# Linear attention and a mixture of experts on one core: another written order for the steps ahead of block 20

## The chip, the core and the metric

The kernel runs on one core of one Trainium2 chip. A core has a matrix engine (PE in the profile, its weight loads PEld), a vector engine (DVE), a scalar engine (ACT), a general engine (POOL) and a queue that issues transfers (SP). Each engine takes its own instructions strictly in the order in which the program was written for it, and they wait for each other by semaphores. The metric is the device time of one execution in microseconds. Three runs of the kernel before gave 652.13, 653.10 and 654.62 us, so its median is 653.1 us.

## The reference, cut to what matters

```python
def phi(x):                                   # 128 random features of a head of 64
    proj = np.einsum('bhsd,md->bhsm', x, omega)
    h = proj - np.sum(x * x, axis=-1, keepdims=True) / 2.0
    return np.exp(h - np.max(h, axis=-1, keepdims=True)) / np.sqrt(m)
q_p, k_p = phi(q_s), phi(k_s)                 # 8 batches, 8 heads, 576 positions
kv = np.einsum('bhsm,bhsd->bhmd', k_p, v)
num = np.einsum('bhsm,bhmd->bhsd', q_p, kv)
den = np.einsum('bhsm,bhm->bhs', q_p, np.sum(k_p, axis=2))[..., None] + 1e-06
x = (num / den) as 4608 tokens of 512
...
e_idx = np.argmax(x @ w_gate, axis=1)         # one of 8 experts for each token
h = np.maximum(x[mask] @ w1[e], 0.0)          # 512 -> 1024
out[mask] = gate_w[mask, None] * eom[mask, e, None] * (h @ w2[e])   # 1024 -> 512
```

## The kernel before

The attention is cut into 32 units. A unit is one head of two batches, so 1152 positions in nine tiles of 128; eight units make a group j of 1152 tokens, and there are four groups. The tokens of all groups are sorted by expert into blocks of up to 128 tokens of one expert; 38 blocks are run in this input. Blocks 0 to 24 are listed after groups 0, 1 and 2 (8, 8 and 9 blocks), so that they can run beside the attention of later groups; the rest is listed after the last group.

Nothing is scheduled by a compiler. The program adds 3310 **steps** to a plan (`plan.add`), each with a key, an engine and a function that emits a few instructions. Two strings of the source then set everything: ORDER names the steps by the number under which they were added, in the order in which they are emitted, and BANKS gives a bank of the accumulator memory (PSUM, eight banks) to each tile that needs one, in that same order. `Plan.order` only asserts that the order keeps every dependency and that no bank is in use twice; `emit` calls the steps in it. So a step's place in ORDER, among the steps of its own engine, is its place in that engine's queue. The 38 blocks run under runtime flags, loaded into registers by steps of their own ("flag").

The steps of a unit u, with k (n = 2u) and q (n = 2u+1) beside each other, g = 0, 1, 2 for three tiles each:

- "ld" (SP): loads of the transposed inputs (L519, tile xt), of the plain ones (xn, from unit 8 on) and of v (L523, rawv). Each has two buffers.
- "hi", "lo", "sqa", "sqr" (ACT L487, POOL L494, ACT L500, DVE L505): halves of the inputs in 16 bits, and squares. For units 0 to 7, "lo" is instead a square in 32 bits (L535 on ACT for unit 0, L537 on POOL for the others).
- "pp" (PE L560): the projections, three tiles of k and of q at a time; it takes two banks. Then "mx", "nb" (DVE L582, L588 to L595) and "ex" (ACT L601): maximum, bias, exponentials; "ex" frees the bank.
- "eh", "el", "eT" (ACT L622, POOL L624, SP L678): halves of the exponentials, and the transposition by the DMA engines. Units 0 to 7 are transposed on PE instead ("tq" L651, "th" L656, "tl" L658).
- "kv", "kvh", "kvs", "kt", "ke", "kg", "gh", "gl" (PE L697, ACT L713 or DVE L715, DVE L717, PE L735, ACT L746, PE L740, ACT L753, DVE L758): keys times values, and their product with the gates.
- "pn" (PE L771; .0 is five tiles, .5 four), "xf" (DVE L780, L782, L784), "xh", "xl", "lga" (DVE L801, POOL L805, POOL L821 or L823), "rows" (SP L844): numerator and denominator, division, halves, gate sums, and the store to memory.

After a group: "route", "counts" (PE L948 to L960), "ranks", "places", "gates", "weigh", "table", "assign", "lists", "pid" (PE L1207), "gi", "controls", "advance", nearly all of them small DVE instructions; and flags.

The steps of a block n: "gx" (POOL L1514) gathers its rows, "xt" (SP L1526) transposes them, "hA" and "hB" (PE L1551, 48 matmuls each) are the two halves of the first layer, "relu" and "rest" (ACT L1558, DVE L1562) split the result, "out" (PE L1582, 12 matmuls a half) is the second layer, "os" (ACT L1637) scales and "put" (POOL L1624) stores. Where a block has another expert than the one before, "bring" (SP L1472) loads 2 MB of weights for each layer and "sw" splits them (ACT L422, DVE L426); n.1 is the first layer, n.2 the second. "w0" and "w0h", "w0l" do this for the first expert.

A step is written below as name.u.g or name.n, as in ex.19.1. The steps that the text speaks of, by their number in ORDER: const.state 6 (four DVE copies of a constant, L388 to L391), w0h.1.0 8, ex.0.1 44, nb.0.1 43, tq.0.0 57, pp.1.1 90, kv.0.0 66, pp.9.2 523, kt.8 498, kvh.8 496, ex.18.0 527, counts.0 1926, hi.11.0 631, ex.19.0 539, ex.19.1 543, pp.10.1 579, kt.9 555, the first flag of ACT and DVE 2046, nb.20.2 591, ex.20.2 592, sqa.12 690, advance.0 2043, pp.11.1 636, kv.15.0 909, hA.4 2284, pp.26.1 1547, pn.24.5 1471, kg.16 976, kv.17.0 1031, xl.28 1720, lga.29 1782, vl.31 1881, gx.21 2554, el.63 1883, eT.31 1884, bring.21.1 2550, hA.21 2556, ld.t.19 1112, eT.16 969, hi.19.0 1115.

Of the kernel before, what the change touches and what calls it, by code (L numbers as in the profile page):

```python
# [128 lines left out]
31 0 3 19 86 1 7 87 4 33 5 34 35 36 88 37 48 49 39 40 50 41 8 38 42 51 52 6 45 46 43 9 53 44 2 10 32 16 13 139 47 11  # L129
57 89 90 66 60 54 55 58 56 63 67 92 95 101 96 102 93 97 94 91 141 68 61 103 64 192 140 22 104 12 59 69 62 105 70 71  # L130
106 72 110 14 73 107 108 65 98 74 99 113 142 100 109 111 114 75 119 79 15 145 146 115 76 77 78 154 155 80 81 82 194
116 120 143 147 20 117 156 121 23 17 112 122 148 157 118 83 149 144 123 124 245 28 125 163 126 164 150 195 151 160 127
158 165 161 152 162 153 132 128 18 198 199 207 133 134 129 169 172 159 84 85 247 130 135 131 166 173 167 174 175 136
208 196 200 170 210 171 211 201 202 176 197 168 246 193 25 298 177 209 21 216 178 179 217 203 248 180 204 205 218 260
213 214 251 206 26 215 212 185 181 225 182 252 183 184 226 300 219 249 222 220 227 29 223 186 221 261 187 228 188 263
229 250 230 262 253 224 254 255 189 138 190 137 351 299 269 231 232 256 270 257 264 233 258 24 266 267 301 238 234 259
304 305 271 239 240 235 241 313 265 268 278 279 280 306 275 302 236 237 314 281 276 353 191 272 282 303 283 273 277
242 352 404 1905 316 317 307 27 308 274 284 318 315 285 286 310 354 309 311 312 287 291 322 331 30 292 319 320 293 288
294 289 323 321 332 325 406 243 333 326 324 290 357 366 367 327 334 355 328 329 368 360 361 330 295 369 356 335 296
244 336 337 358 370 363 364 407 1906 405 457 458 359 338 365 362 339 410 344 340 384 411 372 373 345 346 341 342 412  # L140
374 371 343 419 347 348 349 297 385 386 460 408 375 378 381 350 461 376 387 379 382 420 422 377 380 413 383 423 388
409 462 389 421 459 1907 514 515 390 464 391 463 414 392 416 467 425 393 397 571 572 415 417 428 418 426 398 468 479
394 395 469 427 429 424 437 396 399 430 438 517 439 431 434 432 400 401 480 440 518 403 435 433 519 465 441 483 471
436 442 629 516 470 443 466 520 444 445 487 475 446 521 574 576 575 481 476 484 477 447 472 485 448 473 488 449 577
450 478 474 482 494 451 489 452 453 456 454 1921 522 495 486 490 455 402 528 1922 524 536 1923 491 496 497 1924 525
1925 526 529 685 686 628 1908 573 498 523 1934 530 1935 1936 532 533 540 492 499 527 531 1937 500 1926 1927 541 1928
537 1929 534 2008 501 535 633 2009 502 2010 1938 493 538 2011 542 1930 1939 544 2012 1931 1932 2013 545 1940 2014 546
543 547 631 632 551 552 578 553 539 1941 1942 747 630 2015 1933 634 2016 581 2017 554 582 2018 548 583 579 555 580 556
584 549 557 585 2019 586 2020 2021 2022 589 558 688 503 2023 504 2024 587 2025 559 2026 505 550 2030 2027 506 2028 588
2029 2031 2033 2032 2034 2035 597 2036 590 2037 2044 2045 2216 746 2046 2038 635 507 508 2039 509 2040 591 2041 592  # L150
690 2042 2218 2234 689 2219 807 2214 510 2043 593 601 594 598 638 636 599 602 642 595 600 596 603 608 604 639 691 2215
643 751 511 640 650 605 560 564 609 561 644 565 562 566 563 567 637 610 808 687 2230 641 568 611 645 646 612 692 647
648 613 658 659 651 652 660 654 655 707 656 649 614 2250 513 512 569 606 1909 665 666 615 2217 661 749 653 657 662 667
616 695 696 708 697 668 698 693 2220 663 669 2223 699 700 709 701 710 2221 702 721 607 748 2224 670 2222 752 722 750
570 694 617 621 671 2226 715 703 622 2231 618 672 812 810 619 716 2225 811 704 705 711 706 673 717 712 713 623 620
2235 664 2251 930 868 2246 809 929 2232 869 714 782 719 2227 753 813 624 625 2228 626 720 2229 2266 756 2233 757 768
758 718 759 723 754 674 678 760 679 769 761 770 675 772 762 676 680 2236 755 681 677 682 683 627 771 763 726 2237 871
727 2239 1910 764 765 773 774 728 776 777 766 778 2238 729 724 783 872 775 779 767 725 730 814 815 829 2240 843 780
2241 833 821 817 818 834 822 731 873 2242 874 2247 830 781 732 2243 733 823 819 824 820 734 835 844 739 787 788 735
870 990 2248 2267 2262 991 931 736 740 789 790 831 784 934 737 785 684 786 1052 2252 738 741 742 935 836 832 2244 745  # L160
2282 791 816 792 793 875 2255 2249 2253 825 826 827 794 904 932 828 995 795 837 838 839 2254 743 905 2245 933 744 876
882 840 2263 878 879 841 2256 2258 883 880 884 894 895 890 2257 891 842 2264 992 1113 2278 881 896 996 796 800 885 845
801 797 802 2259 803 798 892 799 846 1056 804 848 806 805 849 893 897 850 851 877 936 993 965 886 852 2268 887 1057
888 951 898 939 2260 853 994 2298 966 854 2265 899 900 889 902 901 855 2269 940 941 952 953 856 2270 2271 937 903 942
955 2272 954 2279 2273 938 2274 1174 2283 1911 2280 2294 847 2284 1117 2285 2299 1051 909 910 947 959 911 948 912 949
943 944 945 2275 2286 913 2287 950 946 914 2276 2314 2261 2277 2281 915 857 861 2290 2288 916 906 956 2289 858 907
2291 957 859 917 960 961 958 2295 862 863 860 864 1118 1026 1112 908 2310 1235 2296 1054 997 998 2300 1055 1000 1004
1005 1006 1001 1002 1016 962 963 2292 1017 1018 1012 1013 1007 1178 999 2301 1003 2303 1008 1020 964 2330 2293 2297
967 1019 1009 865 1010 1021 2302 1179 1022 918 1053 2315 867 968 1011 2304 969 2312 1296 2331 2306 922 970 919 920 921
1014 1015 2305 2311 923 924 925 971 1239 1023 926 928 1943 1944 972 1087 1024 1357 1058 2307 1059 1945 1946 1061 1947  # L170
1956 973 1957 1958 2313 2308 1065 927 1025 1027 866 1948 974 1949 1073 1950 1077 1951 975 1959 1114 1173 2328 1952
2047 1062 1960 1063 1066 1953 2316 1954 2048 1078 1961 1962 1079 2049 1074 1955 1075 2050 1067 1963 1028 1064 1115
1029 1088 1116 1031 1032 976 2317 977 1964 1030 1175 2326 1912 1033 2051 978 2319 1034 2052 2053 2054 2318 1240 2055
2056 1080 1068 1076 2320 1148 2057 979 1060 1035 983 2322 2058 2321 2059 1300 1176 2327 1036 1149 1177 2060 1069 2063
2061 1070 2062 980 984 2064 1081 2065 985 2066 1037 2069 1071 2070 2067 981 2068 2072 982 2073 1038 2323 1418 1234
1295 2071 2074 1039 2075 986 2076 2077 987 2078 2079 2083 2080 1082 2081 1040 1119 1072 2329 2324 1085 1044 1083 1122
1041 1045 1123 1042 1134 1046 1084 2332 988 2309 2346 2362 1124 1047 1043 1048 1301 1089 1125 1120 1086 1121 2335 1126
2333 2082 1127 1128 2334 1138 1139 1130 1135 1140 1131 1136 1142 2085 1361 1129 1049 1090 1092 2347 2084 1479 2342
1091 1093 2338 1237 2336 1137 1141 1143 1144 1094 2337 1238 989 1050 1132 1095 1145 1133 1096 1180 1097 1181 1098 1209
1146 1183 1099 2339 1187 1195 1188 1184 1196 1185 1186 1147 2325 1210 1100 1199 2343 1189 1362 1182 1191 1203 1190  # L180
2340 2348 1105 1236 1356 2344 1913 1422 1150 2378 1151 1197 1200 1192 1193 1198 2345 1106 1204 1201 1205 2349 1206
1202 1298 2360 2363 1540 1152 2358 1299 2350 1423 1483 2351 1153 1154 1101 1417 2379 1601 1102 1107 1108 1103 1104
2354 2352 1270 1194 2353 1155 1156 1271 1241 1157 1207 1158 1208 1256 1244 1242 1159 2355 1248 1160 1249 1250 1245
1246 1257 1260 2359 1161 1109 1247 1251 1211 1110 1212 1358 2374 1162 1166 1167 1261 1262 1258 1163 2361 1263 1259
2356 1214 1168 1215 2364 1169 2365 1216 1164 1165 1170 1217 2376 1213 1297 2394 2341 2357 1243 1218 2367 1302 1219
# [1553 lines left out]
```

## Time and profile before

| | us |
|---|---|
| median of three runs | 653.1 |
| the profiled execution | 655.51 |
| its span, first to last instruction | 653.5 |
| PE busy in the span | 608.4 |
| DVE, ACT, POOL busy | 414.9, 414.5, 339.8 |
| mean granted clock of PE | 0.98 |

The profile is of one execution, 2.4 us above the median. Its page has the busy time of each engine, the granted clock of PE in 40 slices, the chain that ended last, and groups of instructions by line. Behind it stands the trace, which is asked for waits ("engine line waited for: us in total, times, longest us"), for stretches of time (busy time and, in brackets, the number of instructions of each engine; PEclk is the granted share of PE's clock, DMA the mean busy share of the 16 DMA engines) and for single instructions in order of time ("start us, us, engine line op out<-in xcount", with idle time of the engine before it and its releaser in square brackets). A matmul's end is modelled, so short idle times of PE are a little too short.

### The profile page before, as it was taken

What the parts mean: (1) busy time and instruction counts of PE and PEld (TensorE: products, weight loads), DVE (VectorE), ACT (ScalarE), POOL (GpSimd) and SP (SyncE); (2) the same over time, 40 slices, a digit from 0 to 9 for tenths busy, and PEclk for the clock granted to TensorE, in tenths of its full rate; (3) what the DMA queues carried; (4) which work ended last, traced back from release to release, by engine and by line L of the source; (5) the groups of instructions that cost most, each with busy time, mean ns of one, the idle gap of its engine ahead of it and who ended that gap; (6) DMA issues with size and microseconds to landing.
All of it is one profiled execution on the core that took longest, in us unless ns stands there. A gap on an engine that the chain in (4) does not pass through costs nothing. (4 is left out here: it accounts for less than half of the span.)

```text
span 653.5 us, 22348 instructions
## 1 busy us (share of the span) xinstructions
PE 608.4 (93%) x8748; PEld 475.2 (73%) x8748; DVE 414.9 (63%) x1253; ACT 414.5 (63%) x970; POOL 339.8 (52%) x235
## 2 busy tenths in 40 slices
PE   5999977799999999999999899999999899999994
PEld 5898866677776776777767677777777676767673
DVE  4879798767678888666799767662774341070125
ACT  4977697689887967968986687854441341161134
POOL 1233444569883788789867587876321221222111
PEclk9999998599999999999999999999999999999999
DMA  8453669898998988979997958557936855833380
GB/s 290 146 177 116 190 235 250 206 207 265 266 369 201 164 237 243 249 221 256 271 245 192 228 147 182 150 113 171 335 97 180 229 93 101 308 65 90 89 311 16
DMA packets 145893, 129.08 MB, mean 198 GB/s; under 512 B 104270, under 2 KB 127440, under 8 KB 144464
## 3 DMA queue, kind: packets, MB, share of 16 engines
q1 hardware_dynamic: 139760, 107.45, 64.1%
q0 software_dynamic: 5984, 19.72, 8.8%
q8 instruction: 85, 1.39, 0.9%
q14 instruction: 64, 0.52, 0.3%
HBM read 83.86 MB, written 19.30 MB: 158 GB/s over the span
## 5 line engine op out<-in xcount | busy, mean ns | idle before, releaser
L1551 PE MATMUL ph<-xt,w1h 128*128 128x128 f16 (+1 forms) x2432 | 205.5, 217 | 6.2 <-issue 3.7
L1551 PE MATMUL ph<-xt,w1l 128*128 128x128 f16 (+1 forms) x1216 | 200.6, 217 | 3.0 <-issue 1.7
L601 ACT ACTIVATE ef<-pp,nb 128x128 f32<-128x128 f32 x576 | 164.7, 383 | 46.1 <-DVE nb L595 30.1
L1551 PEld LDWEIGHTS <-w1h 128*128 128x128 f16 x2432 | 180.7, 98 | 15.1 <-issue 8.4
L582 DVE TENSOR_REDUCE pp<-pp 128x3 f32<-128x384 f32 x192 | 104.1, 558 | 34.6 <-PE pp L560 24.5
L1562 DVE SCALAR_TENSOR_TENSOR hl<-ph,hh 128x512 f16<-128x512 f32 (+1 forms) x76 | 50.6, 665 | 111.2 <-ACTq L1480 76.3
L1551 PEld LDWEIGHTS <-w1l 128*128 128x128 f16 x1216 | 118.0, 98 | 3.6 <-DVE w1l L426 1.8
L624 POOL TENSOR_TENSOR es<-ef,es 128x1152 f16<-128x1152 f32 x44 | 104.6, 2381 | 18.7 <-ACT es L622 9.9
L1514 POOL DMA_INDIRECT gx<-rows,gi x38 | 40.6, 1068 | 140.8 <-ACT os L1637 110.7
L1582 PE MATMUL po<-w2h,hl 128*128 128x512 f16 x280 | 106.1, 379 | 1.4 <-DVE hl L1562 1.4
L1582 PE MATMUL po<-w2h,hh 128*128 128x512 f16 x280 | 106.3, 380 | 0.7 <-DVE nb L595 0.7
L1582 PE MATMUL po<-w2l,hh 128*128 128x512 f16 x280 | 106.1, 379 | 0.0
L1582 PEld LDWEIGHTS <-hh 128*128 128x128 f16 x560 | 52.0, 99 | 55.3 <-DVE hl L1562 0.9
L1558 ACT ACTIVATE hh<-ph 128x512 f16<-128x512 f32 (+1 forms) x76 | 44.4, 585 | 72.6 <-PE ph L1551 63.7
L494 POOL TENSOR_TENSOR xlo<-xt,xhi 128x1152 f16<-128x1152 f32 x24 | 57.1, 2378 | 21.6 <-ACT xhi L487 19.0
L805 POOL TENSOR_TENSOR xs<-xf,xs 128x576 f16<-128x576 f32 x32 | 41.9, 1312 | 40.2 <-DVE xs L801 17.3
L1637 ACT ACTIVATE os<-po,gx 128x512 f32<-128x512 f32 (+1 forms) x36 | 24.8, 690 | 59.6 <-PE po L1582 59.4
L1582 PEld LDWEIGHTS <-hl 128*128 128x128 f16 x280 | 27.4, 98 | 35.7 <-DVE hl L1562 3.2
L622 ACT CAST es<-ef 128x1152 f16<-128x1152 f32 x44 | 50.9, 1160 | 2.2 <-ACTq L1475 0.7
L560 PE MATMUL pp<-omh,xhi 64*128 64x128 f16 x432 | 42.7, 225 | 7.4 <-DVE xf L784 4.4
L771 PE MATMUL pn<-kvs,et 128*128 128x81 f16 (+1 forms) x960 | 47.4, 208 | 2.2 <-DVE kvs L758 1.6
L771 PEld LDWEIGHTS <-et 128*128 128x128 f16 (+1 forms) x960 | 40.8, 104 | 10.2 <-issue 1.9
(184 smaller groups left out, 1042.7 us busy)
## 6 DMA issues: line engine op xcount, KB each, us to landing
r<-w SPq DMA_DIRECT2D x10, 2048.0 KB, 9.7
xt<-kqt SPq DMA_DIRECT2D x32, 576.0 KB, 6.7
xn<-kqn SPq DMA_DIRECT2D x24, 576.0 KB, 5.7
rawv<-v SPq DMA_DIRECT2D x32, 325.0 KB, 6.0
rows<-xs SPq DMA_DIRECT2D x16, 576.0 KB, 4.9
r<-w SPq DMA_DIRECT2D x8, 512.0 KB, 6.8
ef<-w SPq DMA_DIRECT2D x2, 512.0 KB
et<-w SPq DMA_DIRECT2D x2, 512.0 KB, 6.9
```

The lines of the kernel that those rows point to most:

```text
L494: lambda t0=t0, t1=t1: nc.gpsimd.tensor_tensor(out=xl(u)[:, t0:t1], in0=xt32(u)[:, t0:t1], in1=xh(u)[:, t0:t1], op=ALU.subtract),
L560: nc.tensor.matmul(banks["pp", 2 * u + i, g][:, c, :], x[r, t], w[r, :], start=(a == 0), stop=(a == len(ops) - 1))
L582: nc.vector.tensor_reduce(out=pp[:, 3, 0:3], in_=pp[:, 0:3, :], op=ALU.min, axis=AX.X)
L601: nc.scalar.activation(ef(n)[:, c, :], banks["pp", n, g][:, c % 3, :], AF.Exp, bias=nb(n)[:, c : c + 1], scale=-SK)
L622: nc.scalar.copy(es(slot_es(n))[:, 0], ef(n))
L624: nc.gpsimd.tensor_tensor(out=es(slot_es(n))[:, 1], in0=ef(n), in1=es(slot_es(n))[:, 0], op=ALU.subtract)
L771: nc.tensor.matmul(pn[lo:hi, c - c0, :], a[:, c, lo:hi], w[:, b, :], start=(i == 0), stop=(i == len(ops) - 1))
L805: nc.gpsimd.tensor_tensor(out=x[:, :, P + o : P + o + D], in0=xf(u)[:, :, 0:D], in1=x[:, :, o : o + D], op=ALU.subtract)
L1551: nc.tensor.matmul(ph[:, f4, 0:w_], w[qd][:, kk, fo : fo + P], xt(n)[:, x, 0:w_], start=(a == 0), stop=(a == 3 * KC - 1))
L1558: nc.scalar.activation(hh(n)[:, sl, 0:w_], banks["ph", n, g][:, :, 0:w_], AF.Relu)
L1562: nc.vector.scalar_tensor_tensor(out=hl(n)[:, sl, 0:w_], in0=banks["ph", n, g][:, :, 0:w_], scalar=0.0, in1=hh(n)[:, sl, 0:w_], op0=ALU.ma ...
L1582: nc.tensor.matmul(po, x(n)[:, f, :], w[f // 2][:, f % 2, :], start=(f == 0 and a == 0), stop=(f == FC - 1 and a == 2))
```

## The change

Only the two strings are replaced: 134 lines of ORDER and the four lines of BANKS. No step is added, removed or moved to another engine, and no function is touched; every instruction, its operands and its size stay as they are. Of the 3310 places in the list, 2178 hold another step than before. The first is place 2, the last place 2417 (xl.30); behind it, from the end of the attention on, both lists are the same, and so is the order of the blocks from 20 on. Most steps move a little (5.5 places on average). Counted in each engine's own queue, 137 of PE's 502 steps stand at another place (by 7 at most), 935 of DVE's 1478 (by 26 at most), 355 of ACT's 825 (19), 139 of POOL's 262 (13) and 175 of SP's 305 (14). The banks are dealt out anew along the new order; most tiles follow the same predecessor in their bank.

```diff
 ORDER = """
-31 0 3 19 86 1 7 87 4 33 5 34 35 36 88 37 48 49 39 40 50 41 8 38 42 51 52 6 45 46 43 9 53 44 2 10 32 16 13 139 47 11
...
+31 0 7 1 86 33 5 35 34 36 88 37 48 49 39 40 50 8 41 38 51 42 43 45 46 9 52 44 47 16 3 10 32 19 139 13 4 2 25 87 22 11
...
 BANKS = """
-0123456701234571045627314235610467356412705631427364503126417502746530125631460271034523457612701367204216257301207435
-2127116304504213076235470142657301640235124734016235404201376204157362472430513627015423067460321764103624317250431206
-3740531024306415327041342013650274301420612574236013456012327563076421043763720641325012437614230125341072364224013540
-7126243104351272016507216504716537567652705676576576576576576576576576576576576576576575776576576575776575776576575776
+0123457012635471056347214235610764536427056132437614503726417502746531025631746032104527456312701347052214237601207356
+2112715304604213076234570241567304620135241734601235404201376204153767422430513620715423067461032761043624317260431205
+3740531023406413257041342061350274301420612573264015346012327563076432104763720641235012437614230215341072364224013540
+7216243104352172416512760504716537567652705676576576576576576576576576576576576576576575776576576575776575776576575776
 """
```

What that means around the places where PE waits, written as queues (the steps of one engine in their new order):

```
ACT   before  ... ex.0.0 w0h.1.0 ex.1.1 ex.0.1 ex.0.2 ...        after  ... w0h.1.0 ex.0.0 ex.0.1 ex.0.2 w0h.1.1 ex.1.1 ...
DVE   before  ... nb.1.1 const.state mx.0.2 nb.0.2 nb.0.1 ...    after  ... mx.0.1 nb.0.1 mx.0.2 nb.0.2 w0l.1.0 nb.1.1 ...
PE    before  tq.0.0 pp.1.0 pp.1.1 kv.0.0                        after  pp.1.0 pp.1.1 tq.0.0 kv.0.0
PE    before  kt.8 pp.9.2 kg.8 counts.0                          after  pp.9.2 kt.8 counts.0 kg.8
ACT   before  ... ex.18.1 gate_exps.0 gh.8 ex.18.2 sqa.11 ex.19.1 ex.19.2 hi.11.0 kvh.9 ex.19.0 eh.19
      after   ... hi.11.0 gh.8 gate_exps.0 ex.18.1 ex.18.2 sqa.11 ex.19.1 ex.19.0 ex.19.2 kvh.9 eh.19
ACT   before  hi.12.0 ex.20.1 flag ex.20.2 sqa.12                after  ex.20.1 hi.12.0 sqa.12 flag ex.20.2
PE    before  hA.4 kv.15.0 kv.15.1                               after  kv.15.0 kv.15.1 hA.4
PE    before  pp.26.0 out.13.1 pp.26.1 pn.24.5                   after  out.13.1 pn.24.5 pp.26.0 pp.26.1
PE    before  kv.17.0 kv.17.1 kg.16                              after  kg.16 kv.17.0 kv.17.1
POOL  before  xl.29 el.62 lga.28 vl.31 gx.21 el.63 lga.29        after  vl.31 xl.29 put.17 el.62 gx.21 lga.28 xl.28 lga.29 el.63
```

On SP many loads of inputs stand later than before, behind transpositions that they stood ahead of (ld.t.19, from behind eT.14 to behind eT.16, is one); others stand earlier.

266 rows, old and new, of the table ORDER are left out of this document.

## The prediction

> **What bounds the kernel now.** I read the page's first two parts, then the busy time of four stretches, then who made PE wait, and last the single instructions around the longest of those waits.
>
> ```profile
> PE 608.4 (93%) x8748; PEld 475.2 (73%) x8748; DVE 414.9 (63%) x1253; ACT 414.5 (63%) x970; POOL 339.8 (52%) x235
> ```
>
> PE is busy for 93% of the span. By stretches (length; busy time and count of PE, PEld, DVE, ACT, POOL; granted clock, DMA share, GB/s):
>
> ```profile
> 0.00:95.00 95.00, 84.52 (x1142) 76.43 (x1144) 73.33 (x215) 70.08 (x213) 31.54 (x27) 1.00 0.59 194
> 95.00:136.00 41.00, 31.60 (x399) 27.63 (x399) 33.51 (x155) 30.00 (x87) 22.26 (x14) 0.71 0.88 223
> 136.00:466.00 330.00, 319.16 (x5024) 243.66 (x5024) 235.23 (x761) 253.77 (x587) 250.75 (x162) 1.00 0.87 221
> 466.00:654.00 188.00, 173.16 (x2189) 127.51 (x2187) 72.80 (x124) 60.61 (x86) 35.27 (x33) 0.99 0.55 152
> ```
>
> The change reaches to about 466 us (its last moved step, xl.30, is an instruction of that time); block 21 and all behind it keep their order. Ahead of 466 PE is idle for 10.5 + 9.4 + 10.8 = 30.7 us. Since the matmuls themselves stay, this and the clock are all that the change can work on. The second stretch is the odd one: 9.4 of its 41 us are idle, and the granted clock is 0.71, while DVE, with 33.5 us, is busier than PE. There the first group is routed beside the attention.
>
> ```profile
> PE pp L560 <- DVE omf L383: 5.2, 1, 5.2
> PE pp L560 <- DVE xf L784: 4.4, 3, 2.7
> PE pp L560 <- ACT ef L601: 3.9, 3, 2.4
> ```
>
> These are the longest of PE's waits. The 5.2 us are the first loads, which both orders begin with alike. The other two are projections that wait for a bank: until a division (xf) or exponentials (ef) have read it. Such a wait is a matter of what stands ahead in DVE's or ACT's queue, so an order can remove it.
>
> **The change, part by part.** It adds and removes no instruction, so I go to each place where PE waits for long and follow the new queues with the old durations.
>
> *Start.*
>
> ```profile
> 13.24 0.17 DVE L388 TENSOR_SCALAR cnt<-cft 128x8 f32<-128x8 f32 x1 [1.63 <-DMA cft<-cf]
> ```
>
> const.state waits on DVE for its table until 13.24; nb.0.1 stands behind it, and ex.0.1 behind that:
>
> ```profile
> 14.42 1.66 ACT L601 ACTIVATE ef<-pp,nb 128x128 f32<-128x128 f32 x6 [0.65 <-DVE nb L588]
> ```
>
> pp.1.1 waits for the bank that ex.0.1 reads:
>
> ```profile
> 15.36 0.37 PE L560 MATMUL pp<-omf,xt 64*128 64x128 f32 x1 [1.32 <-ACT ef L601]
> ```
>
> In the new order const.state comes 74 places later and nb.0.1 straight behind its maximum, so these 1.32 us go.
>
> ```profile
> 11.62 0.55 PE L651 MATMUL tq<-ident,ef 128*128 128x128 f32 x3
> 11.94 1.06 ACT L422 ACTIVATE w1h<-r 128x1024 f16<-128x1024 f32 x1 [1.19 <-DMA r<-w]
> ```
>
> tq.0.0 (up to 0.55 us), which filled time ahead of pp.1.0, now stands behind pp.1.1. That leaves 0.8. What is late next is the weight load: w0h.1.0 now stands ahead of ex.0.0 on ACT, and if its 512 KB come no earlier than 11.94, ex.0.0 and pp.1.0 lose what is gained. Its load is issued third instead of seventh, so I take -0.8, between -1.3 and +0.5.
>
> *First routing.*
>
> ```profile
> 103.42 0.30 PE L735 MATMUL kv<-cmt,kvs 128*64 128x128 f16 x4 [0.69 <-DVE kvs L717]
> ```
>
> kt.8's 0.69 us are filled by pp.9.2, which now stands ahead of it.
>
> ```profile
> 109.73 0.89 ACT L601 ACTIVATE ef<-pp,nb 128x128 f32<-128x128 f32 x3 [0.32 <-DVE nb L595]
> 110.49 1.16 ACT L487 CAST xhi<-xt 128x1152 f16<-128x1152 f32 x1
> 111.53 0.30 ACT L713 ACTIVATE kvs<-kv 128x130 f16<-128x130 f32 x1
> 111.70 0.90 ACT L601 ACTIVATE ef<-pp,nb 128x128 f32<-128x128 f32 x3
> ```
>
> ```profile
> 112.66 0.26 PE L560 MATMUL pp<-omh,xhi 64*128 64x128 f16 x1 [2.44 <-ACT ef L601]
> ```
>
> pp.10.1 waits 2.44 us for ex.19.0 (111.70), which hi.11.0 (1.16) and kvh.9 (0.30) precede on ACT. The new order runs hi.11.0 six steps earlier, asks ex.19.1 instead of ex.19.0 for the bank, and puts both ahead of kvh.9.
>
> ```profile
> 103.76 0.27 ACT L746 COPY kvf<-kv 128x128 f32<-128x128 f32 x1 [0.72 <-PE kv L735]
> ```
>
> But ACT has little idle time in these ten microseconds (0.72 here, 0.32 at 109.73), so pp.10.1 starts earlier and kt.9, behind it, waits for kvh.9 and kvs.9 at the end of the same ACT work: most of the wait moves by one step. Counting ACT from kvh.8 on, with hi.11.0 in the 0.72 and ex.19.2 no longer held by its bias for 0.32, I get kt.9 earlier by their sum: -1.0.
>
> ```profile
> 123.33 0.39 PE L560 MATMUL pp<-omh,xhi 64*128 64x128 f16 x2 [2.68 <-DVE xf L784]
> ```
>
> pp.11.1 waits 2.68 us for xf.8.5. DVE loads block flags before it, with 0.87 us of idle time behind them:
>
> ```profile
> 120.83 0.17 DVE L1184 TENSOR_TENSOR rt<-rt,exs 128x8 f32<-128x8 f32 x1 [0.87 <-DVE oi L1245]
> ```
>
> Meanwhile ACT does nothing for 4.35 us, since nb.20.2, which ex.20.2 needs, stands behind the flag on DVE:
>
> ```profile
> 122.69 0.88 ACT L601 ACTIVATE ef<-pp,nb 128x128 f32<-128x128 f32 x3 [4.35 <-DVE nb L595]
> ```
>
> The new order puts nb.20.2 ahead of the flag on DVE and sqa.12 ahead of it on ACT, but the bank of pp.11.1 now follows ex.20.2 instead of advance.0, and ex.20.2 still stands behind ACT's flag. With xf.8.5 behind DVE's flag as before, only part of the 0.87 can go, and I put 0.4 on top of the 1.0. The two together: -1.4 by the sum, between -4 (2.44 and 2.68 both gone but for 1.1) and +1.5 (the new bank's own wait). I take -1.2, as this stretch has the most steps in one another's way.
>
> *Beside the blocks.*
>
> ```profile
> PE ph L1551 <- DVE w1l L426: 1.0, 1, 1.0
> ```
>
> ```profile
> 199.49 1.09 PE L697 MATMUL kv<-vs,es 128*128 128x65 f16 x30
> ```
>
> hA.4 waits 1.0 us for the low halves of its weights; kv.15.0 and kv.15.1 (1.09 us), which ran behind it with their inputs ready, now stand ahead: -0.8, between 0 and -1.1.
>
> ```profile
> 362.48 0.23 PE L560 MATMUL pp<-omh,xhi 64*128 64x128 f16 x1 [1.28 <-DVE xf L784]
> 363.08 0.62 PE L771 MATMUL pn<-kvs,et 128*128 128x81 f16 x12
> ```
>
> pp.26.1 waits 1.28 for xf.24.0; pn.24.5 (0.62) now runs first, of which I count half, since out.13.1 already stood ahead of that wait: -0.3, between 0 and -0.6. PE's other waits here are shorter than these and I leave them.
>
> *What is given back.*
>
> ```profile
> 447.56 1.00 POOL L1514 DMA_INDIRECT gx<-rows,gi  x1
> 448.58 2.39 POOL L624 TENSOR_TENSOR es<-ef,es 128x1152 f16<-128x1152 f32 x1
> ```
>
> el.63 (448.58) releases eT.31 on SP, behind which bring.21.1 loads block 21's weights; the chain of waits gives that load 9.30 us:
>
> ```profile
> 455.44 9.30 DMA r<-w
> ```
>
> PE meets these weights with a wait of 0.23 us, so there is no slack:
>
> ```profile
> 467.29 0.23 PE L1551 MATMUL ph<-xt,w1l 128*128 128x128 f16 x1 [0.23 <-DVE w1l L426]
> ```
>
> Of POOL's steps ahead of el.63, these two besides gx.21 count:
>
> ```profile
> 445.54 0.49 POOL L823 TENSOR_TENSOR lga<-lga,xf 128x144 f32<-128x144 f32 x1
> ```
>
> ```profile
> 440.92 1.28 POOL L805 TENSOR_TENSOR xs<-xf,xs 128x576 f16<-128x576 f32 x1 [1.65 <-DVE nb L595]
> ```
>
> In the new order POOL runs gx.21 (1.00), lga.28 (0.49), xl.28 (1.28) and lga.29 (as lga.28) between el.62, behind which it is free at 445.54, and el.63: 445.54 + 3.26 = 448.8 instead of 448.58, so +0.2 and, with what lies between instructions, +0.3.
>
> *Sum.* -0.8 - 1.2 - 0.8 - 0.3 + 0.3 = -2.8 us. The profiled execution took 655.51 us, 2.4 above the median; I take the difference off the median: 653.1 - 2.8 = **650.3 us**, -0.43%. The bounds of the terms are -7 and +2.3; they are unlikely all at one end, so the forecast's own range is 648 to 652.
>
> **The rivals.** *The half clock goes.*
>
> ```profile
> 102.00:112.00 10.00, 6.22 (x92) 5.46 (x91) 8.98 (x45) 7.42 (x25) 2.51 (x2) 1.00 1.12 208
> 112.00:124.00 12.00, 7.51 (x111) 6.17 (x112) 8.91 (x49) 6.24 (x17) 8.86 (x5) 0.51 0.68 168
> 124.00:129.50 5.50, 5.50 (x54) 5.03 (x50) 4.64 (x21) 4.92 (x12) 2.62 (x4) 0.52 1.13 276
> ```
>
> Behind ten microseconds in which PE was busy for 6.22, the clock is halved from 112 to 129.5. From 124 on PE never waits, so 5.5 us of work would take 2.8; ahead of it the engines around PE set the pace and perhaps 0.8 more would go. If the shorter waits before 112 keep the clock up, that is a further -3.6: 646.7 us. For it: the first routing loses a microsecond of PE idle time ahead of the drop. Against it: most of the wait only moves. Chance 0.20. The Trainium skill ("TensorE: Matmul & The Clock Gate", Part 1) says that the clock falls after an idle window of about 3.4 us and rises after as much sustained work; by that rule no wait shown here would halve it, and the order would not matter to it. The longest wait listed is 2.68 us behind the first, so the trace differs on the fall, and it decides.
>
> *The gain is swallowed.* PE comes to block 21 with 0.23 us to spare. If unit 31 does not move forward with PE (el.63 hangs on POOL, which is busy for 250.75 of the 330 us, 76%), the gain ahead is spent waiting for the weights of that block: 653.0. Against it: el.63's input needs os.18 and ex.63 on ACT, which follow PE. With it goes the case that the waits merely move. Chance 0.15.
>
> *Loads come late (slower).*
>
> ```profile
> 224.29 2.69 SPq L678 DMA_TRANSPOSE et<-es  x1
> ```
>
> The loads of xt, 32 of them, take a median of 6.7 us from issue to landing:
>
> ```profile
> xt<-kqt SPq DMA_DIRECT2D x32, 576.0 KB, 6.7
> ```
>
> ```profile
> 234.42 1.16 ACT L487 CAST xhi<-xt 128x1152 f16<-128x1152 f32 x1
> ```
>
> ld.t.19 now stands behind eT.16 (224.29) on SP, so it is issued at 227.0 at the earliest and lands at 233.7 by the median of 6.7; hi.19.0, which has kept its place, ran at 234.42: 0.7 us are left, where there were 25. ld.n.14, ld.n.22, ld.t.20, ld.v.24 and ld.v.29 come out as tight by the same count. The load's step on ACT holds up everything behind it, relu of the running block too. It decides from a landing of about 7.4 us on; at 8.3 six such waits of 1.2 us cost 7.2: 650.3 + 7.2 = 657.5. For it: DMA is busy for 0.87 over that stretch, and the page shows only the median. Chance 0.17.
>
> **How the numbers follow.** The forecast gets 0.48. Half a per cent is 3.3 us, about what a measurement of this kernel can tell from no change, so faster begins at 649.8, almost at the forecast; I give 0.46 of the forecast's chance to faster. Faster: 0.20 + 0.22 = 0.42. Same: 0.26 + 0.15 = 0.41. Slower: 0.17. The range, 645.0 to 657.0, takes in the half-clock case with 1.7 us below it and all but the far half of the late loads; about 0.15 is left out.
>
> **What would show it.** At 13 us const.state is no longer ahead of nb.0.1 and PE's 1.32 us are gone; the wait of pp.10.1 is under 1 us and a new one of about 2 stands at kt.9; pp.11.1 waits 1 to 2 us for ex.20.2; hA.4's wait is down to about 0.4; hA.21's is up by a few tenths. The stretch to 136 us is shorter by 2, the one from 466 on is the same within 1. I am wrong on the first rival if the granted clock is 1.00 from 112 on, on the second if unit 31's weights make PE wait for over 1 us, on the third if ACT waits for DMA at xhi, sqt or vs.

## The result, and the profile after

The changed kernel took 661.64 us (median of four runs, 660.75 to 664.29), the kernel before 653.59 us in four runs beside it. The ratio is 1.011, with a 95% interval from 1.0078 to 1.0143. So the new order is slower by about 1.1%, where 650.3 us and a range up to 657.0 were predicted.

The profiled execution has a span of 658.3 us, 4.8 more than before. First the busy times of the page, then the four stretches of the prediction (columns as there; the last is longer by the difference of the spans):

```profile
PE 608.6 (92%) x8748; PEld 472.7 (72%) x8748; DVE 422.0 (64%) x1253; ACT 414.6 (63%) x970; POOL 339.3 (52%) x235
```

```profile
0.00:95.00 95.00, 85.11 (x1169) 76.98 (x1170) 74.39 (x227) 72.78 (x221) 34.58 (x27) 1.00 0.58 194
95.00:136.00 41.00, 31.31 (x453) 27.80 (x454) 34.65 (x150) 32.78 (x96) 24.92 (x15) 0.84 0.92 236
136.00:466.00 330.00, 315.58 (x4918) 238.70 (x4916) 237.53 (x750) 247.63 (x571) 243.20 (x159) 0.99 0.88 217
466.00:659.00 193.00, 176.63 (x2217) 129.25 (x2214) 75.42 (x129) 61.45 (x87) 36.59 (x34) 1.00 0.57 152
```

DVE runs the same 1253 instructions and is busy for 422.0 us instead of 414.9. An order cannot change how much work there is, so these 7.1 us are instructions that took longer. The first two stretches got better: PE has run 1142 + 399 = 1541 matmuls by 136 us before and 1169 + 453 = 1622 now. The third gave back more than that: with 5024 matmuls before and 4918 now, PE has run 6565 by 466 us before and 6540 now. Its busy time there is 3.6 us less, and the granted clock 0.99.

I compared the end of each of PE's steps in the two traces, at places up to which both had run the same steps. The changed kernel is ahead by 1.9 us at 84 us (kg.6), by 5.2 at 123 (pn.9.0) and by 7.1 at 247 (pp.19.1). Behind that it loses: it is ahead by 2.6 after out.7.0 (258 us), by 1.0 after counts.2 (349), by 0.6 after out.14.0 (375), and behind by 2.8 at hB.20 (467), by 3.9 after hA.21 and by 5.1 at the end. So some 12 us are lost between 247 us and the end, half of it at two steps: 3.9 at out.7.0 and 2.4 at counts.2. Another 1.1 go at hA.21, and the 3.4 between out.14.0 and hB.20 go in pieces of less than 0.8 us, which no run here takes apart. The list of PE's waits names all three (columns: who waited for whom, us in total, times, longest):

```profile
PE kv L735 <- DVE kvs L717: 2.4, 2, 2.1
PE pos L949 <- DVE r_one L911: 2.2, 1, 2.2
PE po L1582 <- DVE hl L1562: 2.2, 1, 2.2
...
PE ph L1551 <- DMA xt<-gx: 1.4, 1, 1.4
```

The third row is out.7.0, the second counts.2, the last hA.21. The kernel before has no wait of pos for r_one, and in place of the third row it has this one, with no wait at out.7.0:

```profile
PE po L1582 <- DVE hl L1562: 1.4, 2, 0.8
```

Now single instructions in order of time. Of out.7.0's wait, and the clock around it in three pieces of 3.41 us:

```profile
254.12 0.39 PE L1582 MATMUL po<-w2h,hh 128*128 128x512 f16 x1 [2.17 <-DVE hl L1562]
```

```profile
251.72:255.13 3.41, 1.24 (x13) 0.62 (x10) 3.26 (x11) 1.13 (x4) 2.83 (x3) 1.00 0.98 131
255.13:258.54 3.41, 3.41 (x13) 1.01 (x10) 1.55 (x6) 2.83 (x11) 2.80 (x2) 0.50 0.92 190
258.54:261.96 3.42, 3.42 (x51) 2.19 (x51) 2.17 (x7) 2.86 (x8) 1.76 (x1) 1.00 0.99 331
```

PE waits 2.17 us, and in the 3.41 us behind it, though it is busy without a gap, its clock is halved: 13 matmuls, where the next 3.42 us hold 51 (of several sizes). So the wait is paid once as idle time and once more as up to 1.7 us of half speed (half of 3.41). The same happens behind a wait of 1.69 us at pp.26.2, with half clock from 371.2 to 374.6 us.

Why was DVE late? Rows of DVE and POOL that stand next to each other in time, first near 242, then near 344 us:

```profile
242.05 3.18 DVE L801 CAST xs<-xf 128x576 f16<-128x576 f32 x1
242.49 2.38 POOL L624 TENSOR_TENSOR es<-ef,es 128x1152 f16<-128x1152 f32 x1
```

```profile
343.88 3.38 DVE L801 CAST xs<-xf 128x576 f16<-128x576 f32 x1
344.51 2.39 POOL L624 TENSOR_TENSOR es<-ef,es 128x1152 f16<-128x1152 f32 x1
...
348.33 0.19 PE L949 MATMUL pos<-r_one,cmt 128*128 128x72 f16 x1 [2.23 <-DVE r_one L911]
```

These are xh.16 and xh.23, casts of 576 elements. They took 3.18 and 3.38 us, and both end about 0.36 us after POOL's instruction does (242.05 + 3.18 = 245.23 against 242.49 + 2.38 = 244.87; 347.26 against 346.90). All casts of the changed kernel in one row (least, median and greatest duration in ns):

```profile
L801 DVE CAST xs<-xf x32: 474/484/3381, 31.8 to 466.9; 128x576 f16<-128x576 f32 x32
```

The median is 0.48 us. Behind xh.23 stands the rest of the first routing steps of group 2 (the next instruction starts at 347.18), and counts.2 waits for that chain. Behind xh.16 stand xf.17, then bounded.1 (2.78 us, again ending with POOL's), then rest.7.0, for which out.7.0 waits. bounded.1 is no cast, but its 2.78 us follow from the late one: in xh_early and xh_red below, where xh.16 takes 0.97 and 0.74 us, it takes 0.18 and 0.16. The kernel before has the row:

```profile
L801 DVE CAST xs<-xf x32: 479/488/1864, 31.8 to 463.3; 128x576 f16<-128x576 f32 x32
```

One of its casts, xh.13, took 1.86 us beside POOL. An instruction of its routing, of 128x8 elements (L1013), took 3.16 us from 352.20 on, and ended 0.04 us after one of POOL's. The clue was there.

### The profile page after: what moved, and what is told of

It reads as the page before. It is cut to its first block, busy times and chain, and to the rows that moved or that the text cites. A ratio compares the mean times of both kernels' runs of the same rounds, so it can differ in the third digit from the quotient of the medians.

```text
span 658.3 us, 22344 instructions
## 1 busy us (share of the span) xinstructions
PE 608.6 (92%) x8748; PEld 472.7 (72%) x8748; DVE 422.0 (64%) x1253; ACT 414.6 (63%) x970; POOL 339.3 (52%) x235
## 5 line engine op out<-in xcount | busy, mean ns | idle before, releaser
L1582 PE MATMUL po<-w2l,hh 128*128 128x512 f16 x280 | 107.5, 384 | 1.1 <-DVE w2l L426 1.1
L1582 PE MATMUL po<-w2h,hl 128*128 128x512 f16 x280 | 107.5, 384 | 0.1
L771 PE MATMUL pn<-kvs,et 128*128 128x81 f16 (+1 forms) x960 | 45.6, 204 | 3.8 <-DVE xf L784 1.5
L771 PEld LDWEIGHTS <-et 128*128 128x128 f16 (+1 forms) x960 | 39.3, 101 | 11.5 <-issue 2.8
```

What stands on the lines that cost most here:

```text
L771: nc.tensor.matmul(pn[lo:hi, c - c0, :], a[:, c, lo:hi], w[:, b, :], start=(i == 0), stop=(i == len(ops) - 1))
L1582: nc.tensor.matmul(po, x(n)[:, f, :], w[f // 2][:, f % 2, :], start=(f == 0 and a == 0), stop=(f == FC - 1 and a == 2))
```

## The experiments

**Theory one**: the first 240 us of the new order are a gain. Behind that, casts of DVE come up while POOL is working; each waits until POOL has a gap (just when it comes through is told in the last section), steps behind it come late, PE waits for over 2 us, and the clock is halved behind such waits. A second and smaller loss lies at block 21. **Rivals**: (a) a lead is swallowed later whatever the order; (b) the waits come from other steps of the queues, and the long casts are slack; (c) the half clock has nothing to do with PE's idle time.

The runs below were made in five jobs, each on another chip. The kernel before took 647.6 to 648.2 us in four of them; in the one of before_again to cut240_red it took 654.3, like the 653.6 above. Why the chips differ is open. So ratios to the kernel before of the same job are compared, not times.

| run | order | ratio to before | 95% interval |
|---|---|---|---|
| cut136 | changed to 137 us, then before | 0.998 | 0.995 to 1.001 |
| cut240 | changed to 240 us, then before | 0.997 | 0.993 to 1.001 |
| cut335 | changed to 330 us, then before | 1.011 | 1.007 to 1.015 |
| rev240 | before to 248 us, then changed | 1.014 | 1.009 to 1.019 |
| cut420 | changed to 421 us, then before | 1.018 | 1.013 to 1.023 |
| xh_early | changed, four casts earlier | 1.004 | 1.0005 to 1.007 |
| xh_early_tail | the same, before from 421 us on | 0.999 | 0.996 to 1.002 |
| xh_red | changed, casts of another form | 1.002 | 0.999 to 1.005 |
| after_again | changed | 1.009 | 1.006 to 1.013 |
| fill | changed, with idle matmuls | 1.013 | 1.006 to 1.020 |
| cut240_red | as cut240, casts of another form | 0.996 | 0.993 to 0.9995 |
| after_b | changed | 1.024 | 1.021 to 1.027 |
| xh_red_b | as xh_red | 1.001 | 0.998 to 1.005 |
| cut240_red_b | as cut240_red | 0.999 | 0.996 to 1.002 |
| warm | as cut240_red, with idle matmuls | 1.002 | 0.9995 to 1.005 |
| xt21 | as xh_red, one transfer moved | 0.998 | 0.995 to 1.001 |
| before_red | before, casts of another form | 1.0005 | 0.998 to 1.003 |

**Where it is lost.** Four kernels take one list up to a step and the rest of the steps in the other list's order (banks dealt out to match):

```diff
 ORDER: cut136, cut240, cut335
-3310 steps in the changed order
+the changed order up to pp.12.2 / pp.19.0 / kt.23, the steps left in the order before
 ORDER: rev240
-3310 steps in the changed order
+the order before up to pp.19.0, the steps left in the changed order
```

> The changed order up to pp.12.2 (about 137 us), the order before behind it. In the two traces PE stands 5.0 us earlier at that place in the changed kernel. Theory one (the new order gains ahead of 245 us and loses behind it): 648 to 650 us, -5 of 653.6. Theory two (a gain of the first part is swallowed by what comes later, whatever the order, since block weights or loads set the pace): 652.5 to 654.

> The changed order up to pp.19.0 (240.5 us, where PE stands 7 us earlier than before), the order before behind it. Theory one: 646 to 649 us, with no PE wait over 2 us ahead of out.7.0 and no half clock between 130 and 640 us. Theory two: 652 to 654, the lead melting between 240 and 470 us at waits for weights or loads.

> The changed order up to kt.23 (330.5 us, lead 3.2 us in the trace, after out.7.0 has waited and the clock has been halved for 3.4 us), the order before behind it. Theory one: 650 to 651, with the wait of out.7.0 and its half clock there, and those near 346 and 370 us gone. If the loss lies in the last part alone (block 21's load and xt.21 behind a weight load): also about 650, but with the lead still there at 400 us. Theory two: 653 to 655.

> The order before up to pp.19.0 (248 us), the changed order behind it. Theory one: the changed part behind 245 us loses by itself what the trace shows, 7 + 5 = 12 us, so 662 to 666 if the same casts fall behind POOL's instructions again; 655 to 658 if the meeting of the two engines depends on the lead that the first part has. Theory two: 653 to 655, as a lead that isn't there can't be lost.

cut136 and cut240 come out 0.2 and 0.3% below before, with intervals that just take in 1; cut335 and rev240 are over 1% above it. cut335 was expected below before and missed. All four are of one job. So the loss lies behind 240 us, and most of it ahead of 330, as cut335 is 1.4% slower than cut240. The gains of the first two are smaller than the 5 and 7 us of lead in the first pair of traces. But the leads were smaller on this chip too: against rev240, which has the order before up to there, cut136 is ahead by 3.1 us at hA.0 and cut240 by 4.2 at pp.19.0. The intervals of the two ratios reach to gains of 3.2 and 4.5 us, so whether rival (a) takes a part of the lead stays open. rev240 shows that the lead is not needed for the loss. In the trace of cut335 out.7.0 waits 2.16 us and out.10.0 2.83 us, each with half clock behind it (3.4 and 6.8 us). xh.16 took 3.16 us there and xh.20 5.06; rev240 has 5.06 and 3.37 us for xh.20 and xh.23.

**The casts.** Two ways to mend them: move four of them ahead, or write the same copy as another form of instruction, in the same place of the queue. Two more kernels tell the part of the last stretch:

```diff
 ORDER: xh_early
-... xf.16.5 advance.1.step.2 gl.17 ... advance.1.step.7 xh.16 ...
+... xf.16.5 xh.16 advance.1.step.2 gl.17 ... advance.1.step.7 ...
 (xh.19, xh.20 and xh.23 in the same way)
 xh_red
-nc.vector.tensor_copy(xs(pr).bitcast(F16)[:, :, o : o + D], xf(u)[:, :, 0:D])
+nc.vector.tensor_reduce(
+    out=xs(pr).bitcast(F16)[:, :, o : o + D], in_=xf(u)[:, :, 0:D].unsqueeze(3), op=ALU.max, axis=AX.X
+)
 ORDER: cut420, xh_early_tail
+the order before for the steps left at pn.28.0
```

> The changed order with four of DVE's casts, xh.16, xh.19, xh.20 and xh.23, moved ahead in the list to the place straight behind their second xf; nothing else. Theory one (a cast that becomes ready for issue while POOL runs an instruction waits until POOL has a gap, so xh.16 and xh.23 took 3.2 and 3.4 us instead of 0.48 in the changed kernel, xh.20 5.1 us in two of the first experiments, and the second layers of blocks 7 and 10 and counts.2 wait for them): the casts take 0.5 us (up to 1.9 where POOL is busy), the waits over 2 us at out.7.0, out.10.0 and counts.2 go down, with the half clock behind them; ratio to before 1.000 to 1.005 instead of 1.011. Rival (the waits come from other steps of the queues, rest.7.0 behind too many maxima, and the long casts are slack): ratio stays at 1.009 to 1.014.

> The changed order as it is, all 32 casts xh written as a maximum over an axis of one element, the form of instruction of sqr, which no trace here shows stretched beside POOL. Theory one: every xh takes 0.6 to 0.75 us whether POOL is busy or not, none over 1 us; ratio 1.000 to 1.006. If every instruction of DVE that reads and writes SBUF is held up by POOL, some xh still take 2 to 5 us and the ratio stays at 1.010 or above. The longer casts by themselves cost 32 times 0.2 us of DVE, off PE's path.

> The changed order up to pn.28.0 (421 us), the order before behind it, with el.63, bring.20.2 and xt.21 as before. Theory one has two parts of loss behind 240 us, the casts, and the weights and rows of block 21 (hA.21 waited 1.37 us in the changed kernel and 3.12 in the kernel with the changed order behind 248 us only); this undoes the second alone: ratio 1.005 to 1.009. If the last part is no loss of its own (its waits only take up what came late): 1.010 to 1.014.

> Both of these edits: the four casts early, and the order before behind pn.28.0. Theory one: all of the loss behind 240 us goes, ratio 0.994 to 0.999, near the 0.997 of the kernel with the changed order up to 240 us. Rival (other steps): above 1.004.

xh_early: the four casts took 0.97, 1.29, 1.72 and under 0.8 us, no half clock stands between 123 and 460 us, ratio 1.004. xh_red: no cast over 0.76 us, 1.002. Rival (b) asked for 1.009 or more and falls. cut420 missed its expectation with 1.018. Its trace has xh.16, xh.20 and xh.23 at 3.17, 5.06 and 3.39 us, and where the orders meet at 421 us another cast is held, xh.27 with 3.21 us (0.48 in the changed kernel). The changed kernel did not run in that job, so what undoing the last part saved there can't be told. With the casts mended the last part is worth 650.16 - 647.29 = 2.9 us (xh_early against xh_early_tail, which has the same long xh.27), though the intervals overlap.

On chips where before takes 648 us, the changed kernel itself had not run by then. It did in a later job, beside xh_red:

> The changed kernel, unchanged, as the control of this chip: ratio to before 1.008 to 1.016.

> The changed order with all casts xh as maxima over one element, beside the changed kernel on one chip. If the casts that wait for POOL are the loss: ratio 0.998 to 1.003, 0.8 to 1.4% below the changed kernel. If they are half of it or less: 1.004 or above.

after_b took 663.12 us (ratio 1.0238, interval 1.0206 to 1.027), xh_red_b 648.50 (1.0014, interval 0.9982 to 1.0046): 14.6 us for the form of 32 small instructions, with every step in its place. That is more than the 0.8 to 1.4% expected, as the changed kernel itself came out above its 1.008 to 1.016. As both have one order, PE's steps can be compared one by one: xh_red_b is ahead by 1.0 us at pp.19.0, by 6.9 after out.7.0, by 12.2 after out.10.0, by 15.3 after counts.2 and by 16.0 after hA.21. So 12.0 of the 16.0 us come up at just the three steps (4.0, 5.3 and 2.7) that wait behind xh.16, xh.20 and xh.23. First the casts of after_b, then those of xh_red_b:

```profile
L801 DVE CAST xs<-xf x32: 474/484/5065, 32.5 to 467.0; 128x576 f16<-128x576 f32 x32
```

```profile
L801 DVE TENSOR_REDUCE xs<-xf x32: 739/743/754, 32.5 to 449.7; 128x576 f16<-128x576 f32 x32
```

The other form takes 0.26 us more each, and none was held up, in the same order and beside the same POOL. xh.20 of after_b shows how long a hold can last; the cast, then POOL's instructions of that time:

```profile
299.54 5.07 DVE L801 CAST xs<-xf 128x576 f16<-128x576 f32 x1
```

```profile
298.14 2.40 POOL L494 TENSOR_TENSOR xlo<-xt,xhi 128x1152 f16<-128x1152 f32 x1
300.48 2.39 POOL L624 TENSOR_TENSOR es<-ef,es 128x1152 f16<-128x1152 f32 x1
302.81 1.43 POOL L645 TENSOR_TENSOR vs<-rawv,vs 128x650 f16<-128x650 f32 x1
304.68 1.28 POOL L805 TENSOR_TENSOR xs<-xf,xs 128x576 f16<-128x576 f32 x1 [0.44 <-DVE xs L801]
```

Three instructions of POOL follow each other with no gap, and the cast, issued during the first, comes through only when the third has ended at 304.24. The Trainium skill ("SBUF — State Buffer", section "Who interferes with whom") says that a DVE cast in a 2-port mode and a GpSimd instruction exclude each other for a whole instruction, and that a tensor_reduce never contends on trn2. Both rows agree with it, though no view here names the mode of the cast, and the hold of 5.07 us is longer than any one of POOL's instructions.

The other part of the difference is the clock. after_b, behind the waits of out.10.0:

```profile
300.96:304.37 3.41, 1.58 (x29) 1.00 (x27) 3.41 (x1) 2.00 (x4) 3.28 (x2) 1.00 0.93 335
304.37:311.19 6.82, 5.82 (x29) 2.62 (x28) 3.12 (x13) 2.43 (x9) 3.60 (x2) 0.50 0.70 227
```

after_b has half clock behind the waits of out.7.0, out.10.0 and counts.2, for 3.4, 6.8 and 6.8 us; xh_red_b has none between 122 and 456 us.

**Is it PE's idle time that halves the clock?**

```diff
 fill (the changed kernel)
+34 matmuls ident16 x ident16 ahead of kv.18.0, 40 ahead of pp.23.1, into columns that are written anew behind them
 warm (cut240_red)
+34, 10 and 40 such matmuls behind pp.10.1, pp.10.2 and pp.11.0, into columns of pp that nothing reads
```

> The kernel before, unchanged, for a trace on the chip of the later runs. Theory one (the first 240 us of the changed order are a real gain): PE stands 4 to 7 us later here at pp.12.2 and pp.19.0 than in the runs that have the changed order there, with about 17 us of half clock near 112 us instead of 10 to 14. Rival (on this chip there is little to gain, as its kernel before is 6 us faster already): later by 0 to 3 us.

> The changed kernel, unchanged, on the chip of the later runs, as their control. From the parts: 1.011 for the first half cut at 335, 1.018 for the one cut at 421: 1.012 to 1.020. Long casts xh.16 (about 3.2 us) and xh.20 or xh.23 or both (3 to 5 us).

> The changed kernel with 34 and 40 matmuls of 128 columns that nothing reads, put ahead of kv.18.0 and pp.23.1, that is into about 2.0 and 2.4 us of the time in which PE waits for rest.7.0 and rest.10.0; the casts stay as long as they are. If the clock is halved for a stretch of 3.41 us after each such stretch in which PE was busy for less than about 0.6: no half clock behind these two places, out.7.0 and out.10.0 take 2.8 us without their waits, and the time is 2 to 5 us below that of the changed kernel on this chip. If the halving doesn't come from PE's idle time: half clock there as before, and the time the same or up to 2 us longer.

> The changed order up to 240 us, the order before behind it, and all casts xh as maxima over one element. Theory one: the casts of the order before that still wait for POOL (4.4 us above their least in the run of this order) go, no xh over 0.8 us; ratio to before 0.990 to 0.996, below both kernels. If the long casts of this order are off PE's path: 0.996 to 0.999, as without this edit.

fill told nothing: in after_again neither place had half clock without the matmuls, and xh.20 was not held up on that chip, so that the second filling stood where PE had no wait. after_again itself, expected at 1.012 to 1.020 and measured at 1.009, was of use in another way. Its out.7.0 waits as long as in the first trace, and no half clock follows:

```profile
254.81 0.39 PE L1582 MATMUL po<-w2h,hh 128*128 128x512 f16 x1 [2.16 <-DVE hl L1562]
```

```profile
250.00:253.41 3.41, 2.24 (x51) 1.99 (x48) 3.38 (x7) 2.88 (x6) 3.19 (x2) 1.00 0.96 218
253.41:256.82 3.41, 2.01 (x10) 0.95 (x11) 2.25 (x9) 1.50 (x6) 3.04 (x2) 1.00 0.98 156
```

All of the half-clock stretches ahead of 600 us in the 20 traces last 3.41 us or a multiple of it, and within a trace their edges lie on one grid of 3.41 us, whose phase differs from execution to execution. In the first trace the wait fell into one piece of that grid, in which PE was busy for 1.24 us of 3.41; here the edge at 253.41 cuts it, which leaves 2.24 and 2.01 us. From its first matmul to its last, out.7.0 took 4.36 us there and 2.76 here.

before_again, a single run, stands in for the kernel before on that chip: after_again leads it by 4.4 us at pp.19.1, by 1.5 after out.7.0, and is behind from counts.2 on, so the picture of the first pair repeats with a smaller lead. Then the direct test, on the half clock of the first routing:

> The changed order up to 240 us, the order before behind it, casts as maxima: ratio 0.993 to 0.997, with the interval below 1.

> The kernel cut240_red_b with 34, 10 and 40 matmuls of 128 columns that nothing reads, behind pp.10.1, pp.10.2 and pp.11.0, where PE then waits 2.16, 0.57 and 2.58 us. If half clock comes from stretches in which PE is busy for less than about 0.6: the half clock near 110 us is gone or down to 3.4 us from 13.65, and the time is 1 to 4 us below cut240_red_b, as the matmuls behind kv.10.0 run at full clock. If the stretch is set by DVE and ACT whatever PE's clock: no half clock, the same time within 1 us. If the filling holds up the maxima that read the same bank: 1 to 4 us longer, shown by DVE waiting for PE behind pp.10.1 and pp.11.0.

First cut240_red_b, then warm, from 108.37 us on:

```profile
108.37:111.78 3.41, 2.05 (x42) 1.68 (x41) 3.31 (x16) 2.07 (x6) 2.60 (x2) 1.00 0.79 207
111.78:122.02 10.24, 6.13 (x76) 5.31 (x71) 9.31 (x45) 6.44 (x17) 7.83 (x6) 0.50 0.97 232
```

```profile
108.37:111.78 3.41, 2.85 (x55) 2.31 (x52) 3.29 (x16) 1.90 (x6) 2.77 (x2) 1.00 0.78 209
111.78:122.02 10.24, 6.95 (x130) 6.07 (x131) 9.31 (x45) 6.53 (x17) 7.69 (x6) 1.00 0.88 234
```

With PE kept busy the half clock is gone, in the whole trace up to 511 us, where each of the other 19 traces has 10.2 to 17.1 us of it near 110 us: rival (c) falls. And it brought nothing there: pp.11.2 ends at 125.22 us with the filling and at 125.27 without. The columns of DVE, 3.3 of 3.41 and 9.31 of 10.24 us busy in both, speak for DVE as what sets the pace of this stretch. The times are 649.61 us with the filling and 646.75 without; their ratios have overlapping intervals, and there is no gain in any case.

**What is left.**

```diff
 ORDER: xt21 (on xh_red)
-... bring.21.1 bring.20.2 xt.21 ...
+... bring.21.1 xt.21 bring.20.2 ...
 before_red: the order before with the casts of xh_red
```

> The changed order with all casts as maxima, and xt.21 (the transposition of block 21's rows) ahead of bring.20.2 (a load of weights) on SP again; nothing else. If the place behind the load is what delays the rows: hA.21 waits less than 0.5 us for them, and the ratio is 0.995 to 0.999, 0.2 to 0.5% below xh_red (1.0019 and 1.0014). If POOL's gather or el.63 delays them: hA.21 still waits over 1.4 us and the ratio stays at 1.000 to 1.003.

> The order before, with all casts as maxima over one element. Its casts were 3 us above their least in all, with little behind them in PE's waits: ratio 0.997 to 1.001. If the casts held PE up here too: 0.990 to 0.996.

The moved transfer is not the cause that I took it for: hA.21 still waits.

```profile
460.50 0.27 PE L1553 MATMUL ph<-xt,w1h 128*128 128x128 f16 x2 [1.69 <-DMA xt<-gx]
```

The ratio, 0.998, cannot be told from that of xh_red. Of the nine profiles with the changed last part eight have a wait of 1.4 to 3.1 us at hA.21, in rev240 for weights and in the others for the rows (fill has none); xh_early_tail and cut420, with the last part of before, have none. Which of its moves does it stays open: el.63, the rows stored by rows.13, and the weights ahead were not tried alone. before_red, 1.0005, shows no gain from the other form of cast in the order before, where few casts met POOL. cut240_red was below before by its interval in one job (0.996) and not, as was expected, in the other (0.999), so no version here is shown to beat the kernel before.

## Why the prediction was wrong, point by point

**The step that failed** is the one on which the whole sum stood: to "follow the new queues with the old durations". The prediction looked at the places where PE waited before and asked what the new order does there. It did not ask which instructions of DVE the new order sets beside POOL's. Durations that depend on the neighbour, 3.18 and 3.38 us for 0.49, made waits of 2.17 and 2.23 us at out.7.0 and counts.2, where before had none of note, and the first of them halved the clock as well. The two steps cost 6.3 us of PE's lead; together with out.10.0 they cost 12.0 us in after_b against xh_red_b. No term of the sum and no rival had this.

- *Start, -0.8.* Right in sign and too small. pp.1.1 no longer waits for ex.0.1, and PE leads by 1.9 us behind tq.0.0 and still at kg.6.
- *First routing, -1.2.* Right in sign. pp.10.1's wait is gone and kt.9 waits 2.15 us, as foreseen. pp.11.1 still waits 2.68 us for xf.8.5, not for ex.20.2. The lead grows by 2.8 us (from 2.4 at kv.8.0 to 5.2 at pn.9.0), but by about 0.6 (1.6 to 2.2) on the chip of before_again, where both have 13.65 us of half clock from 114 and 110 us on. Much of the difference of the first pair is thus the clock (24 us of it before, 13.65 after). Against rev240 it grows by 0.0 to 0.4 in cut136, cut240 and cut335, all four with 13.65 us of half clock near there, so at the same clock the term was too large.
- *hA.4, -0.8.* Right: the lead grows from 5.2 to 5.9 us.
- *pp.26.1, -0.3.* The wait is gone, but pp.26.2 waits 1.69 us for its exponentials right behind it, with 3.4 us of half clock.
- *el.63, +0.3.* Too small: hA.21 waits 1.37 us instead of 0.23. I had followed POOL's queue to el.63, and not bring.20.2, which moved ahead of xt.21 on SP; xt21 shows that this was not the whole cause either.
- *Rival "the half clock goes", 646.7.* Wrong in its price, 3.6 us (its own parts, 2.7 and 0.8, make 3.5). warm removed the half clock of the first routing and won nothing there; DVE is busy for over 90% of it. The row that PE "never waits" from 124 us on was read as if all that PE did faster would count. And it was half clock elsewhere, newly made, that counted.
- *Rival "the gain is swallowed".* Not what happened: the lead was lost ahead of block 21, and more than the lead. Whether a part of a lead is swallowed stays open, as cut136 and cut240 had led by 3.1 and 4.2 us only.
- *Rival "loads come late".* The sign was right and the reason wrong. (By its own slack of 0.7 us a landing of 8.3 makes waits of 0.9, not 1.2, so 5.4 instead of 7.2.) The only wait of ACT on inputs that is new is this one:

```profile
ACT sqt L500 <- DMA xn<-kqn: 0.5, 1, 0.5
```

The forecast of -0.4% is near what the first 240 us alone gave (0.997, with an interval that takes in 1). That is luck in part: the start gained more than its term and the first routing less. Behind that place the terms were -0.3 and +0.3, and what they left out came to 12 us.

## What to carry to other kernels

Before a reordering is priced with old durations, look at the least, median and greatest duration of every line: where the greatest is several times the median, a neighbour may be the reason, and the new neighbour has to be looked up. Here the casts of DVE beside a busy POOL were such a line, with 1.86 us against 0.49. Where one stands in a chain that PE waits for, a slower form that was held up in none of seven traces (0.74 against 0.48 us) was worth 2%. And a wait of PE of 2 us cost up to 1.7 us more by the clock at out.7.0, while a halved clock in a stretch where DVE was busy for over 90% cost nothing.

## What the runs showed of the hardware

In these traces the clock of PE changes only at the edges of a grid of 3.41 us, and each execution places the grid anew. Over the 20 traces, from 20 to 600 us, I took for each piece of the grid at full clock the share in which PE was busy. Under 0.45 the next piece was at half clock in 30 of 31 cases, from 0.45 to 0.63 in 33 of 102, from 0.63 on in 1 of 3129. At half clock it stayed so in 43 of 43 cases under 0.8, and came back in 52 of 53 from 0.95 on. The Trainium skill ("TensorE: Matmul & The Clock Gate", Part 1) has the free-running window and an idle window that halves the clock; the traces agree with the window, and show that a piece only half idle is enough. So the same wait of 2.17 us was followed by 3.41 us of half clock in one execution and by none in another, and out.7.0 took 4.36 and 2.76 us.

In the 13 traces with casts, 52 casts take over 0.9 us, and each of them ends 0.35 to 0.36 us behind the end of one of POOL's instructions. That need not be the first: xh.20 of after_b was passed by two more and took 5.07 us. Nor does POOL need a gap: in 22 of the 52 its next instruction follows without one. What decides which of POOL's instructions pass a waiting cast is not shown. And the two sorts of chip jobs, with 648 and 654 us for the same kernel before, differed in which casts were held up: xh.20 took 5.07 us in after_b and 0.74 in after_again, and the changed kernel stood at 1.024 and 1.009. What sets the two apart is not shown.
